# A retention, mixture-of-experts and Mish kernel: x's rows at one place in 256 bytes, one weight rounded later, Mish in the first activation

## The chip, the cores and the metric

The kernel runs on one core of a Trainium2 chip. The metric is device time in microseconds: the median of the runs, 616.08 us before the change (3 runs, 615.87 to 616.91).

## What is computed

Three stages follow each other; all data are float32 (two inputs of the last stage come as float64).

```python
# 2 batches, 8 heads, 576 positions, 64 dims
scores = scale * np.matmul(q, k.transpose(0, 1, 3, 2))
ret = scores * Dmat[None, :, :, :]          # gamma_h ** (i - j) for i >= j, else 0
attn = np.matmul(ret, v)
x = attn.transpose(0, 2, 1, 3).reshape(1152, 512)
...
for e in range(4):                          # w1[e] 512x1024, w2[e] 1024x512
    h = np.maximum(x @ w1[e], 0.0)
    out += p[:, e:e + 1] * (h @ w2[e])
...
h = out @ w_in                              # 512x2048
g = h * np.tanh(np.log1p(np.exp(np.minimum(h, 20.0))))   # Mish; h itself inside tanh for h > 20
return g @ w_out                            # 2048x512
```

## The kernel before

**Precision.** Every operand of the feed-forward stages is kept as two float32r parts, a rounded high part (ScalarE, a Copy) and the remainder (source minus high part, VectorE or GpSimd). A product of two operands takes three matmuls: high by high, low by high, high by low.

**Retention** (lines 248 to 476) goes through 8 units, each one batch and two heads. For unit u PE makes the scores (L317), the products with v of unit u-1 (L385), the states of the chunks (L351), the last scores (L339), and then `cross(u-1)` (L370, L375), which adds the states' part to the output of unit u-1. `chain(u)` makes the decayed states `sbd`: ScalarE copies the first (L355), VectorE adds the other three (L357). `place_x` and `rest_x` (L395, L402, L407) write the unit's output into x, high and low. Behind the loop stands `cross(7)`, for the last unit. While this goes on, the first weights are prepared: `weight_task` takes the next entry of a list of tasks, which is either the four sums for a weight G (GpSimd, L138 to L141, in place in the raw buffer) or the split of a weight (high part on ScalarE, L162; remainder, L166, in four pieces on GpSimd or in one on VectorE).

**Feed-forward.** The 4 experts make 8 units u = 0 to 7 of 512 hidden columns, and the Mish stage 4 more, u = 8 to 11 (`NE` is 8). Of the 1152 tokens 1024 go in two blocks of 512 and 128 apart. For each unit the list `seq` sets the order:
- S(u,c), c = 0 or 1: the first matrix product, `first_pair`, for 256 hidden columns. The 2x2 block product is done with seven products in place of eight, from sums of x (`xop`, 7 sums of 2 row blocks, high and low) and sums of weights (O as loaded, G summed). One product is 6 matmuls (L227) of 128x128 weights over 512 columns of x. Products 1, 5, 7, 6, 2, 4, 3 accumulate in four PSUM banks; three of them are copied out on ScalarE (L238) before their bank is used on, GpSimd adds two of these (L616, L617), VectorE adds the sums into the banks (L593), and `hidden` turns each finished bank into h: Relu or Mish with a Copy on ScalarE (L570; L566, L567), remainder on VectorE (L571; L568). A bank may be opened by the next S when its remainder is done. S(0,0) runs as `first_plain`, with eight products.
- L(u,c): the same for the last 128 tokens (L655, `xc` stationary), T(u) their second product.
- Y(u,c,tb): the second product (L671 for the experts, L687 for the Mish stage), 24 matmuls of 512 columns, added into `acc`.

The first S of the Mish stage, S(8,0), takes the products in the order 1, 5, 7, 3, 6, 2, 4, since the sums of x for it come late. Then follow L(8,1), S(8,1), Y(8,0,0), Y(8,1,0), S(9,0), L(9,0), Y(8,0,1), Y(8,1,1), T(8) and S(9,1).

The engines' orders are as written: each engine takes its instructions in the order in which the Python code issues them. Behind every step but S, `feed_forward` calls `task` once (`catch_up` gives another number and engine at some steps), and a list `later` puts some tasks into the middle of the next S, behind product 7. Raw weights are loaded by the SyncE queue (`load_w`, L130) into three buffers, each load waiting until the buffer's last reader is done; the float64 weights of the Mish stage are turned into float32 on VectorE and ScalarE (L507 to L533) between the rest and go out to DRAM and back.

The lines that the change touches: the tile of x (L197 to L199, SBUF padded to 32 bytes), the dummy activation before the first matmul (L416), the task of unit 6 of retention (L459), `hidden` (L563 to L573), `first_pair` (L609 to L632), and `task` and `catch_up` (L803 to L852).

Of the kernel before, what the change touches and what calls it, by code (L numbers as in the profile page):

```python
# [77 lines left out]
def f32(ap):  # L78
    return ap.bitcast(F32)
# [3 lines left out]
def retention_moe_mish(ctx: ExitStack, tc: tile.TileContext, kq_in, kv_in, probs, w1, w2, w64, cdec, out):  # L83
# [112 lines left out]

    xop = keep.tile([P, 2, 7, 2, TB + 16], F32R, tag="x", name="x")[..., :TB]  # L197
    xc = keep.tile([P, 2, NPAIR, LT], F32R, tag="xc", name="xc")
    p_last = keep.tile([P, E], F32, tag="pl", name="pl")  # L199

# [47 lines left out]
    with ExitStack() as actx:  # L248
# [160 lines left out]
        def retention():  # L409
# [4 lines left out]
            for i, val in enumerate((-896.0, 255.0, 255.0 * 2 ** 23)):  # L414
                dve.memset(cbias[:, i:i + 1], val)
            act.activation(out=acc[:, 0, :1], in_=cbias[:, :1], func=AF.Copy)  # L416
            warm = ps_tile()
# [8 lines left out]
            for u in range(NUN):  # L426
# [30 lines left out]
                if u == 3:  # L457
                    sp.dma_start(out=p_dram.rearrange("e (n t) -> n e t", t=PT), in_=pt)
                for _ in range({2: 1, 5: 1, 6: 1}.get(u, 0)):  # L459
                    weight_task(u - NUN - 2, pool)  # L460
# [101 lines left out]

    def hidden(u, out, src):  # L563

        if u >= NE:
            act.activation(out=src, in_=src, func=AF.Mish)  # L566
            act.activation(out=out[:, 0], in_=src, func=AF.Copy)  # L567
            dve.tensor_tensor(out=out[:, 1], in0=src, in1=f32(out[:, 0]), op=ALU.subtract)  # L568
            return
        act.activation(out=out[:, 0], in_=src, func=AF.Relu)  # L570
        dve.scalar_tensor_tensor(  # L571
            out=out[:, 1], in0=src, scalar=0.0, in1=f32(out[:, 0]), op0=ALU.max, op1=ALU.subtract
        )  # L573

# [12 lines left out]
    def first_pair(u, c, behind, later, order, sum_at=7):  # L587

        o = [[bank(t, j) for j in range(2)] for t in range(2)]
        h = [h_tile(u, c, i) for i in range(2)]  # L590

        def add(out, a, b):
            dve.tensor_tensor(out=out, in0=a, in1=b, op=ALU.add)  # L593

        done = {}
        for n in order:
            done[n] = product(u, c, n, o)
            if n == 1:
                p1 = copy_sum("p1", sums, done[n])
            elif n == 5:  # L600
                p5 = copy_sum("p5", sums, done[n])
            elif n == 7:
                p7 = copy_sum("p7", ph, done[n])
                if 2 in done:
                    hidden(u, h[0][:, :, 0], done[2])
            elif n == 6:
                p16 = sum_tile("p16", ph)
                add(p16, done[n], p1)
            elif n == 2 and 7 in done:  # L609
                if 3 in done:  # L610
                    add(done[3], done[3], p16)
                hidden(u, h[0][:, :, 0], done[2])
                if 3 in done:
                    hidden(u, h[1][:, :, 0], done[3])
            if n == sum_at:
                pool.tensor_tensor(out=p5, in0=p5, in1=p7, op=ALU.add)  # L616
                pool.tensor_tensor(out=p5, in0=p5, in1=p1, op=ALU.add)  # L617
            if n == 7:
                while later:
                    later.pop(0)()  # L620
            for f in behind.get(n, ()):
                f()
            if n == 4:
                add(done[4], done[4], p16)
                hidden(u, h[0][:, :, 1], done[4])
            if len(done) == 7:
                if n == 3:
                    add(done[3], done[3], p16)
                add(done[6], done[6], p5)
                if n == 3:  # L630
                    hidden(u, h[1][:, :, 0], done[3])
                hidden(u, h[1][:, :, 1], done[6])  # L632

# [148 lines left out]
    def feed_forward():  # L782
# [19 lines left out]
        for i, (m, u, *at) in enumerate(seq):  # L802
            def task(n=1, lo_engine=pool):  # L803
                for _ in range(n):
                    weight_task(i, lo_engine)

            if m == "S":
# [13 lines left out]
                elif (u, c) == (0, 1):  # L821
                    later.append(lambda: task(2))
                elif u == NE:
                    later.append(lambda: task(1))
                    later.append(lambda: task(2, dve))
                elif c == 1:
                    later.append(task)
                if (u, c) == (0, 0):
                    first_plain(u, c, behind)
                    task(2)  # L830
                else:
                    first_pair(u, c, behind, later, order, sum_at)
# [15 lines left out]

            catch_up = {("Y", 0, 0, 0): (2, dve), ("L", 1, 0): (1, dve), ("Y", 0, 0, 1): (2, pool)}
            catch_up |= {("Y", NE, 0, 0): (2, dve), ("L", NE + 1, 0): (1, dve), ("Y", NE, 0, 1): (2, dve)}  # L850
            if m != "S" and i != i_x and not i_x + 2 <= i <= i_x + 4:
                task(*catch_up.get(seq[i], (1, pool)))  # L852
            if m != "S":
# [68 lines left out]
```

## Time and profile before

| | |
|---|---|
| median of 3 runs | 616.08 us (615.87 to 616.91) |
| the profiled execution | 615.17 us |
| its span | 613.3 us |
| PE matmul busy | 601.5 us, 98% |
| PE weight loads busy | 500.7 us, 82% |
| VectorE (DVE) busy | 430.6 us, 70% |
| GpSimd (POOL) busy | 368.7 us, 60% |
| ScalarE (ACT) busy | 310.6 us, 51% |

A busy time of PE holds the overlap and the waits between pipelined matmuls, so 98% does not say how fast the matmuls follow each other: their pace is read from their starts. Times in the rows are microseconds from the span's start. In a timeline row stand the start, the length, the engine, the line, the operation, out<-in, the shape and the number of merged instructions, and in brackets how long the engine stood idle before and what ended that.

### The profile page before, as it was taken

How to read it: one execution, taken by the hardware profiler on the slowest of the kernel's cores; microseconds unless marked ns; L12 is line 12 of the kernel's file. 1: busy time of each engine (PE TensorE's matmuls, PEld its weight loads, DVE VectorE, ACT ScalarE, POOL GpSimd, SP SyncE). 2: the span in 40 equal slices, each digit the busy share in tenths (PEclk: the TensorE clock that was granted, in tenths of full speed). 3: DMA queues.
4: the chain of work that ended last, by engine and by line, in shares of the span. 5: the costliest groups of instructions: out<-in, count | busy, mean ns of one | idle time of the engine just before them, and what ended most of it. 6: DMA issues, size and time to landing. Idle time of an engine off the chain costs nothing.

```text
span 613.3 us, 8553 instructions
## 1 busy us (share of the span) xinstructions
PE 601.5 (98%) x3189; PEld 500.7 (82%) x3189; DVE 430.6 (70%) x568; ACT 310.6 (51%) x472; POOL 368.7 (60%) x413
## 2 busy tenths in 40 slices
PE   8979999999999999999999999999899999999997
PEld 7968888888888888888888888888778788888886
DVE  3857569779779779779779879769566867344133
ACT  3646356455455546546545545425656665345130
POOL 2471738948848847857856856773551775854300
PEclk9989999999999999999999999999999999999999
DMA  8934213532631632631632641631220541220023
GB/s 336 397 105 118 90 34 124 180 109 91 203 119 56 203 120 70 223 120 52 204 122 69 214 116 67 187 71 52 61 77 12 194 120 53 85 69 1 0 69 120
DMA packets 56801, 72.30 MB, mean 118 GB/s; under 512 B 31160, under 2 KB 38456, under 8 KB 56760
## 3 DMA queue, kind: packets, MB, share of 16 engines
q1 hardware_dynamic: 56616, 71.46, 36.4%
q8 instruction: 25, 0.41, 0.3%
q10 hardware_dynamic: 144, 0.29, 0.1%
q14 instruction: 16, 0.13, 0.1%
HBM read 57.57 MB, written 14.17 MB: 117 GB/s over the span
## 4 chain that ended last, share of the span: by engine, by line
PE 83%; DMA 5%; POOL 4%; DVE 3%; issue 2%; ACT 2%; SPq 0%; POOLq 0%; DVEq 0%
PE b L227 33%; PE ps L671 28%; PE ps L687 17%; PE ps L655 5%; DMA kq<-kq_in 2%; DMA wr<-w 2%; POOL w L166 1%; DMA cst_sb<-cdec 1%; DMA w<-w 1%; POOL p L616 1%; POOL x L728 1%; POOL qg L302 0%; DVE acc L745 0%; ACT h L567 0%; DVE ps L744 0%
## 5 line engine op out<-in xcount | busy, mean ns | idle before, releaser
L166 POOL TENSOR_TENSOR w<-wr,w 128x256 fp32r<-128x256 f32 x252 | 214.0, 882 | 135.1 <-ACT w L162 135.1
L227 PE MATMUL b<-x,w 128*128 128x512 f32 x1014 | 240.8, 395 | 2.0 <-DVE h L568 1.6
L227 PEld LDWEIGHTS b<-x,w 128*128 128x128 f32 x1014 | 190.3, 188 | 47.2 <-DVE h L568 2.5
L671 PE MATMUL ps<-h,w 128*128 128x512 f32 x768 | 177.0, 389 | 0.0
L671 PEld LDWEIGHTS ps<-h,w 128*128 128x128 f32 x768 | 143.2, 188 | 29.4 <-issue 0.3
L687 PE MATMUL ps<-w,h 128*128 128x512 f32 x384 | 88.6, 390 | 0.2 <-POOL w L166 0.2
L162 ACT ACTIVATE w<-wr 128x1024 fp32r<-128x1024 f32 x71 | 73.8, 1053 | 27.3 <-POOL wr L141 27.0
L687 PEld LDWEIGHTS ps<-w,h 128*128 128x128 f32 x384 | 71.6, 188 | 15.2 <-POOL w L166 0.6
L238 ACT ACTIVATE p<-b 128x512 f32<-128x512 f32 x69 | 40.6, 598 | 52.9 <-PE b L227 52.7
L570 ACT ACTIVATE h<-b 128x512 fp32r<-128x512 f32 x64 | 38.0, 597 | 56.4 <-DVE b L593 44.2
L571 DVE SCALAR_TENSOR_TENSOR h<-b,h 128x512 fp32r<-128x512 f32 x64 | 42.8, 689 | 30.1 <-ACT h L570 28.5
L616 POOL TENSOR_TENSOR p<-p,p 128x512 f32<-128x512 f32 x23 | 34.2, 1486 | 22.6 <-ACT p L238 22.6
L593 DVE TENSOR_TENSOR b<-b,p 128x512 f32<-128x512 f32 x69 | 45.7, 691 | 2.5 <-POOL p L617 2.0
L744 DVE TENSOR_TENSOR ps<-ps,pb 128x1024 f32<-128x1024 f32 x28 | 34.4, 1229 | 16.5 <-PE ps L671 16.4
L568 DVE TENSOR_TENSOR h<-b,h 128x512 fp32r<-128x512 f32 x32 | 22.1, 691 | 30.4 <-ACT h L567 30.4
L519 ACT ACTIVATE e<-e,cbias 128x512 uint32<-128x512 uint32 x32 | 23.0, 718 | 34.1 <-DVE e L507 34.1
L655 PEld LDWEIGHTS ps<-w,xc 128*128 128x128 f32 x288 | 37.2, 188 | 1.9
L655 PE MATMUL ps<-w,xc 128*128 128x256 f32 x288 | 37.8, 280 | 0.0
L530 DVE SCALAR_TENSOR_TENSOR g<-w,g 128x512 f32<-128x512 uint32 x32 | 36.0, 1125 | 0.0
L745 DVE TENSOR_TENSOR acc<-acc,ps 128x1024 f32<-128x1024 f32 x28 | 34.2, 1221 | 1.0
L687 PE MATMUL ps<-w,hl 128*128 128x512 f32 x144 | 34.6, 389 | 0.0
L593 DVE TENSOR_TENSOR p<-b,p 128x512 f32<-128x512 f32 x23 | 15.8, 685 | 26.0 <-PE b L227 19.7
(79 smaller groups left out, 596.8 us busy)
## 6 DMA issues: line engine op xcount, KB each, us to landing
wr<-w SPq DMA_DIRECT2D x32, 512.0 KB, 5.2
w<-w SPq DMA_DIRECT2D x32, 512.0 KB, 4.5
O<-g SPq DMA_DIRECT2D x16, 256.0 KB, 5.4
W<-g SPq DMA_DIRECT2D x16, 256.0 KB, 4.7
wr<-O SPq DMA_DIRECT2D x8, 512.0 KB, 3.5
wr<-W SPq DMA_DIRECT2D x8, 512.0 KB, 3.5
kq<-kq_in SPq DMA_DIRECT2D x7, 576.0 KB, 9.2
kv<-kv_in SPq DMA_DIRECT2D x7, 544.0 KB, 9.3
```

The source lines that it names most:

```text
L162: act.activation(out=w[:, 0], in_=t, func=AF.Copy)
L166: lo_engine.tensor_tensor(out=w[:, 1, k], in0=t[:, k], in1=f32(w[:, 0, k]), op=ALU.subtract)
L227: pe.matmul(o[t][j], w[:, a, 2 * kh + kk, fb * P:(fb + 1) * P], xop[:, b, r, kk], start=opens and i == 0, stop=i == 5, skip_group_check=no ...
L238: act.activation(out=t, in_=src, func=AF.Copy)
L530: dve.scalar_tensor_tensor(out=g, in0=lo_w, scalar=2.0 ** -52, in1=g, op0=ALU.mult, op1=ALU.add)
L570: act.activation(out=out[:, 0], in_=src, func=AF.Relu)
L571: dve.scalar_tensor_tensor(out=out[:, 1], in0=src, scalar=0.0, in1=f32(out[:, 0]), op0=ALU.max, op1=ALU.subtract)
L593: dve.tensor_tensor(out=out, in0=a, in1=b, op=ALU.add)
L616: pool.tensor_tensor(out=p5, in0=p5, in1=p7, op=ALU.add)
L655: pe.matmul(o, xc[:, b, k], w[:, a, k], start=k == 0 and n == 0, stop=k == 3 and n == 2)
L671: pe.matmul(o[:, j], w[:, a, d:d + P], h[:, b, f], start=i == f == n == 0, stop=i == f == 1 and n == 2,)
L687: pe.matmul(o[:, n], h, w[:, b, f * DM:(f + 1) * DM], start=k == f == i == 0, stop=k == f == 1 and i == 2,)
```

## The change

It does five things.
1. The tile of x loses its 16 elements of padding per row (2112 bytes become 2048), and `p_last`, 16 bytes padded to 32, is allocated ahead of it. In the built program x's rows start at 192, 0, 64 and 128 past a multiple of 256 bytes before, and all at 224 now; `xc` goes from 192 to 224. The weights, h, `hl` and `acc` lie at 224 before and after.
2. The split of the weight G of S(0,1), the third weight in the list of tasks, moves from unit 6 of retention to behind the last `rest_x`.
3. The dummy activation at the start is Mish in place of Copy; the program then has one ACT_TABLE_LOAD, where it had two.
4. `hidden` is cut into a high part (ScalarE) and a low part (VectorE). In S(8,0) alone this gives another order: VectorE's adds into the banks of products 4 and 6 come before the low parts of the banks of 3 and 4. The other S keep their order.
5. `task` takes a list of engines. Behind Y(8,0,0) one of two remainders goes to GpSimd, behind L(9,0) and Y(8,0,1) all of them; before they went to VectorE.

```diff
-    xop = keep.tile([P, 2, 7, 2, TB + 16], F32R, tag="x", name="x")[..., :TB]
+    p_last = keep.tile([P, E], F32, tag="pl", name="pl")
+    xop = keep.tile([P, 2, 7, 2, TB], F32R, tag="x", name="x")
     xc = keep.tile([P, 2, NPAIR, LT], F32R, tag="xc", name="xc")
-    p_last = keep.tile([P, E], F32, tag="pl", name="pl")
...
-            act.activation(out=acc[:, 0, :1], in_=cbias[:, :1], func=AF.Copy)
+            act.activation(out=acc[:, 0, :1], in_=cbias[:, :1], func=AF.Mish)
...
-                for _ in range({2: 1, 5: 1, 6: 1}.get(u, 0)):
+                for _ in range({2: 1, 5: 1}.get(u, 0)):
                     weight_task(u - NUN - 2, pool)
...
             rest_x(NUN - 1)
+            weight_task(-1, pool)
...
-    def hidden(u, out, src):
+    def hidden_high(u, out, src):
         if u >= NE:
             act.activation(out=src, in_=src, func=AF.Mish)
             act.activation(out=out[:, 0], in_=src, func=AF.Copy)
+        else:
+            act.activation(out=out[:, 0], in_=src, func=AF.Relu)
+
+    def hidden_low(u, out, src):
+        if u >= NE:
             dve.tensor_tensor(out=out[:, 1], in0=src, in1=f32(out[:, 0]), op=ALU.subtract)
...
+            elif n == 2 and 3 in done:
+                add(done[3], done[3], p16)
+                h2, h3 = (u, h[0][:, :, 0], done[2]), (u, h[1][:, :, 0], done[3])
+                hidden_high(*h2)
+                hidden_high(*h3)
+                hidden_low(*h2)
             elif n == 2 and 7 in done:
-                if 3 in done:
-                    add(done[3], done[3], p16)
                 hidden(u, h[0][:, :, 0], done[2])
-                if 3 in done:
-                    hidden(u, h[1][:, :, 0], done[3])
...
             if n == 4:
                 add(done[4], done[4], p16)
-                hidden(u, h[0][:, :, 1], done[4])
+                h4, h6 = (u, h[0][:, :, 1], done[4]), (u, h[1][:, :, 1], done[6])
+                hidden_high(*h4)
+                hidden_low(*(h3 if 3 in done else h4))
             if len(done) == 7:
...
-                hidden(u, h[1][:, :, 1], done[6])
+                hidden_high(*h6)
+                if n == 4:
+                    hidden_low(*h4)
+                hidden_low(*h6)
...
-            def task(n=1, lo_engine=pool):
-                for _ in range(n):
+            def task(*engines):
+                for lo_engine in engines or (pool,):
                     weight_task(i, lo_engine)
...
-                    later.append(lambda: task(1))
-                    later.append(lambda: task(2, dve))
+                    later.append(lambda: task(pool, dve, dve))
...
-            catch_up = {("Y", 0, 0, 0): (2, dve), ("L", 1, 0): (1, dve), ("Y", 0, 0, 1): (2, pool)}
-            catch_up |= {("Y", NE, 0, 0): (2, dve), ("L", NE + 1, 0): (1, dve), ("Y", NE, 0, 1): (2, dve)}
+            catch_up = {("Y", 0, 0, 0): (dve, dve), ("L", 1, 0): (dve,), ("Y", 0, 0, 1): (pool, pool)}
+            catch_up |= {("Y", NE, 0, 0): (dve, pool), ("Y", NE, 0, 1): (pool, pool)}
```

How it moves the instructions, at the three places that count. On ACT, at the end of retention, before (`sbd_107` is the state tile of the last unit, `w` and `wr` the split and the raw weight):

```order
L402 ACTIVATE xc<-acc 128x128
L402 ACTIVATE x<-acc 128x512
L162 ACTIVATE w<-wr 128x1024
L355 ACTIVATE sbd_107<-b_606 128x64
L395 ACTIVATE acc<-ps 128x576
...
L722 ACTIVATE x<-acc 128x2x512 x3
```

And on ACT at the same place now:

```order
L402 ACTIVATE xc<-acc 128x128
L402 ACTIVATE x<-acc 128x512
L355 ACTIVATE sbd_107<-b_600 128x64
L395 ACTIVATE acc<-ps 128x576
L402 ACTIVATE x<-acc 128x512
...
L162 ACTIVATE w<-wr 128x1024
L738 ACTIVATE x<-acc 128x1024 x3
```

The copy L162 has moved from ahead of `sbd` to behind the unit's placing, ahead of the first three high parts of x's sums (L722 before, L738 now).

On DVE in S(8,0) before, from the add of products 6 and 1 on (`b_3864`, `b_3866`, `b_3865` and `b_3867` are the banks of h2, h3, h4 and h6):

```order
L593 TENSOR_TENSOR b_3866<-b_3866,p_3914 128x512
L568 TENSOR_TENSOR h<-b_3864,h 128x512
L568 TENSOR_TENSOR h<-b_3866,h 128x512
L593 TENSOR_TENSOR b_3865<-b_3865,p_3914 128x512
L568 TENSOR_TENSOR h<-b_3865,h 128x512
L593 TENSOR_TENSOR b_3867<-b_3867,p_3886 128x512
L568 TENSOR_TENSOR h<-b_3867,h 128x512
```

The same stretch of DVE now:

```order
L602 TENSOR_TENSOR b_3866<-b_3866,p_3914 128x512
L574 TENSOR_TENSOR h<-b_3864,h 128x512
L602 TENSOR_TENSOR b_3865<-b_3865,p_3914 128x512
L574 TENSOR_TENSOR h<-b_3866,h 128x512
L602 TENSOR_TENSOR b_3867<-b_3867,p_3886 128x512
L574 TENSOR_TENSOR h<-b_3865,h 128x512
L574 TENSOR_TENSOR h<-b_3867,h 128x512
```

Each add of a bank now stands ahead of the low part of the bank before it; ACT's order there is the same but for the table load.

On POOL from S(8,1) to S(9,0) and on, before (`wr` the sums of a G in place, `p` the sums of copied products):

```order
L166 TENSOR_TENSOR w<-wr,w 128x256 x4
L138 TENSOR_TENSOR wr<-wr 128x2x128
...
L617 TENSOR_TENSOR p_4165<-p_4165,p_4157 128x512
L138 TENSOR_TENSOR wr<-wr 128x2x128
L139 TENSOR_TENSOR wr<-wr 128x2x128
L140 TENSOR_TENSOR wr<-wr 128x2x128
L141 TENSOR_TENSOR wr<-wr 128x2x128
L166 TENSOR_TENSOR w<-wr,w 128x256 x8
```

And on POOL now:

```order
L141 TENSOR_TENSOR wr<-wr 128x2x128
L166 TENSOR_TENSOR w<-wr,w 128x256 x4
L138 TENSOR_TENSOR wr<-wr 128x2x128
...
L628 TENSOR_TENSOR p_4168<-p_4168,p_4160 128x512
L166 TENSOR_TENSOR w<-wr,w 128x256 x8
L138 TENSOR_TENSOR wr<-wr 128x2x128
L139 TENSOR_TENSOR wr<-wr 128x2x128
L140 TENSOR_TENSOR wr<-wr 128x2x128
L141 TENSOR_TENSOR wr<-wr 128x2x128
L166 TENSOR_TENSOR w<-wr,w 128x256 x8
```

Four pieces have come ahead of the second group of sums, and eight (two weights) ahead of the third, behind the sums of S(9,0)'s products; three L166 of 128x1024 have gone from DVE.

## Rows read from the trace of the kernel before

**Rows 1.** Waits of PE: line waited for, us in total, times, longest us.

```profile
PE ps L370 <- ACT sbd L355: 3.7, 1, 3.7
...
PE ps L687 <- POOL w L166: 0.2, 1, 0.2
```

**Rows 2.** Stretches of 1 us: busy us of each engine, then TensorE's granted clock.

```profile
39.00:40.00 1.00, 0.00 (x0) 0.00 (x0) 0.00 (x0) 0.69 (x1) 0.28 (x1) 1.00 0.00 0
...
41.00:42.00 1.00, 1.00 (x14) 1.00 (x12) 0.96 (x4) 0.65 (x2) 1.00 (x3) 0.50 0.00 0
```

**Rows 3.** Timeline, the end of retention, ACT, DVE and PE.

```profile
34.23 0.61 ACT L402 ACTIVATE x<-acc 128x512 fp32r<-128x512 f32 x1
...
35.85 1.09 PE L385 MATMUL ps<-ret,kv 128*64 128x128 f32 x16
...
39.31 1.06 ACT L162 ACTIVATE w<-wr 128x1024 fp32r<-128x1024 f32 x1 [4.47 <-POOL wr L141]
...
40.51 0.91 DVE L357 SCALAR_TENSOR_TENSOR sbd<-sbd,cst_sb,b 128x64 f32<-128x64 f32 x3 [5.21 <-ACT sbd L355]
...
40.62 1.76 PE L370 MATMUL ps<-qg,sbd 64*64 64x128 f32 x16 [3.68 <-ACT sbd L355]
...
42.52 9.24 PE L227 MATMUL b<-x,w 128*128 128x512 f32 x36
```

**Rows 4.** Timeline of PE from S(1,0) on, and the page's group of L227.

```profile
77.85 9.89 PE L227 MATMUL b<-x,w 128*128 128x512 f32 x42
...
87.58 1.57 PE L655 MATMUL ps<-w,xc 128*128 128x256 f32 x12
...
88.99 11.05 PE L671 MATMUL ps<-h,w 128*128 128x512 f32 x48
...
99.88 0.39 PE L687 MATMUL ps<-w,hl 128*128 128x512 f32 x1
...
L227 PE MATMUL b<-x,w 128*128 128x512 f32 x1014 | 240.8, 395 | 2.0 <-DVE h L568 1.6
```

**Rows 5.** Timeline, S(8,0) to S(8,1), ACT, DVE and PE.

```profile
426.90 1.28 ACT L566 ACT_TABLE_LOAD   x1
...
429.07 0.58 ACT L566 ACTIVATE b<-b 128x512 f32<-128x512 f32 x1 [0.89 <-PE b L227]
...
431.66 2.95 PE L227 MATMUL b<-x,w 128*128 128x512 f32 x12
431.96 0.69 DVE L568 TENSOR_TENSOR h<-b,h 128x512 fp32r<-128x512 f32 x1 [0.70 <-ACT h L567]
...
433.29 0.58 ACT L566 ACTIVATE b<-b 128x512 f32<-128x512 f32 x1 [1.36 <-DVE b L593]
...
434.53 0.69 DVE L568 TENSOR_TENSOR h<-b,h 128x512 fp32r<-128x512 f32 x1 [1.28 <-ACT h L567]
...
435.28 1.66 PE L227 MATMUL b<-x,w 128*128 128x512 f32 x6 [0.67 <-DVE h L568]
...
437.86 5.82 PE L227 MATMUL b<-x,w 128*128 128x512 f32 x24 [0.92 <-DVE h L568]
```

**Rows 6.** Timeline, Y(8,0,1) to S(9,1), with POOL's eight pieces of L166 twice.

```profile
469.81 2.00 ACT L162 ACTIVATE w<-wr 128x1024 fp32r<-128x1024 f32 x2
...
477.07 0.74 POOL L138 TENSOR_TENSOR wr<-wr 128x256 f32<-128x256 f32 x1 [14.44 <-DVE w L166]
...
479.64 5.73 PE L227 MATMUL b<-x,w 128*128 128x512 f32 x24
...
480.63 1.06 ACT L162 ACTIVATE w<-wr 128x1024 fp32r<-128x1024 f32 x1 [3.44 <-POOL wr L141]
...
481.77 7.43 POOL L166 TENSOR_TENSOR w<-wr,w 128x256 fp32r<-128x256 f32 x8 [1.17 <-ACT w L162]
...
485.82 4.41 PE L227 MATMUL b<-x,w 128*128 128x512 f32 x18 [0.45 <-ACT p L238]
...
527.11 5.63 POOL L166 TENSOR_TENSOR w<-wr,w 128x256 fp32r<-128x256 f32 x8 [1.17 <-ACT w L162]
```

More of the change, by code (lines that the diff above doesn't have):

```diff
@@ L567, in hidden @@
             act.activation(out=out[:, 0], in_=src, func=AF.Copy)
+        else:
+            act.activation(out=out[:, 0], in_=src, func=AF.Relu)
+    def hidden_low(u, out, src):
+        if u >= NE:
             dve.tensor_tensor(out=out[:, 1], in0=src, in1=f32(out[:, 0]), op=ALU.subtract)
[L569 to L573, printed above, removed]
+        else:
+            dve.scalar_tensor_tensor(
+                out=out[:, 1], in0=src, scalar=0.0, in1=f32(out[:, 0]), op0=ALU.max, op1=ALU.subtract
+            )
+    def hidden(*args):
+        hidden_high(*args)
+        hidden_low(*args)
     def first_plain(u, c, behind):
@@ L821, in feed_forward @@
                 elif (u, c) == (0, 1):
-                    later.append(lambda: task(2))
+                    later.append(lambda: task(pool, pool))
                 elif u == NE:
-                    later.append(lambda: task(1))
-                    later.append(lambda: task(2, dve))
+                    later.append(lambda: task(pool, dve, dve))
                 elif c == 1:
@@ L829, in feed_forward @@
                     first_plain(u, c, behind)
-                    task(2)
+                    task(pool, pool)
                 else:
@@ L847, in feed_forward @@
             ahead = i + 1 < len(seq) and seq[i + 1][0] == "S"
-            catch_up = {("Y", 0, 0, 0): (2, dve), ("L", 1, 0): (1, dve), ("Y", 0, 0, 1): (2, pool)}
-            catch_up |= {("Y", NE, 0, 0): (2, dve), ("L", NE + 1, 0): (1, dve), ("Y", NE, 0, 1): (2, dve)}
+            catch_up = {("Y", 0, 0, 0): (dve, dve), ("L", 1, 0): (dve,), ("Y", 0, 0, 1): (pool, pool)}
+            catch_up |= {("Y", NE, 0, 0): (dve, pool), ("Y", NE, 0, 1): (pool, pool)}
             if m != "S" and i != i_x and not i_x + 2 <= i <= i_x + 4:
-                task(*catch_up.get(seq[i], (1, pool)))
+                task(*catch_up.get(seq[i], ()))
             if m != "S":
```

## The prediction

> **What bounds the kernel now.** I read the list of waits first. In a span of 613.3 us TensorE (PE) waits long only once, 3.7 us at the end of retention, for `sbd` of ScalarE (ACT); its shortest listed wait is 0.2 us for a weight of GpSimd (POOL) [rows 1]. So PE is the bound, and a change pays only where it shortens PE's own work, or one of its few waits. Second, the clock in small windows: behind the 3.7 us the granted clock is 0.50, which is the 1.2 GHz level, where 1.00 (2.4 GHz) stood before [rows 2]; that wait costs more than its length. Third, the timeline, read for PE's pace. From the first of 42 matmuls of L227 (x moving) to the next row 9.73 us pass, 231.7 ns each; from the first of 48 of L671 (h moving) to the next row 10.89 us, 226.9 ns [rows 4]. Both move 512 columns over a 128x128 weight tile and wait for nothing. What differs is where the moving rows lie: in the built program the weights and h start 224 bytes past a multiple of 256, x's rows at 192, 0, 64 and 128, since a row is 528 elements long. Last, the timeline around the other waits [rows 5, 6].
>
> **Part A, x's place.** With rows of 512 elements and `p_last` ahead, all rows of x begin at 224. No instruction is added or moved. The nearest row for a matmul with both operands at 224 is L671, with the same form and type, so I take its pace: 231.7 - 226.9 = 4.8 ns less, times the 1014 matmuls of L227 [rows 4], 4.9 us, all on the path. The ends: 0 if the place is not the cause (below), and 6 us if x gets a nanosecond below h. `xc` moves from 192 to 224 as well, as the stationary operand of L655: 1.41 us for 12, 117.5 ns [rows 4]. At the 2.4 GHz level 256 columns take 106.7 ns and 512 take 213.3, so L655 has 10.8 ns beyond its columns, L671 13.6; L655 has nothing to give by that comparison. I take 0, with 0.7 us (half of the 4.8 ns on 288) as the end.
>
> **Part B, G(0,1) rounded behind retention.** ACT's copy L162 of that weight stands ahead of L355, which starts `sbd` of the last unit. It idles 4.47 us for POOL's sums and runs from 39.31 to 40.37; L355 follows, DVE's three L357 start at 40.51, and PE's L370 at 40.62 [rows 3]. Without it, L355 runs when ACT has done L402 at 34.84: 0.21 us more, then 0.91 of L357, so `sbd` is there by 36.0. PE's L385 ends at 35.85 + 1.09 = 36.94 [rows 3]. So L370 starts there, 40.62 - 36.94 = 3.7 us sooner, 0.9 us behind its operand. The clock then has no reason to fall: L370 and L375 (40.62 to 42.52, 1.90 us at half clock) save 0.95, and the 36 matmuls from 42.52, 9.24 us where 35 x 0.2317 + 0.395 = 8.50 would do, save 0.74 [rows 2 to 4]. B is 3.68 + 0.95 + 0.74 = 5.4 us. The ends: 4.4, if the clock falls for another reason, and 5.8. The moved copy (1.06 us) now stands on ACT ahead of the three L722 that round T1, T3 and T2; those wait for DVE's L713, which needs the last x, so they lose nothing. POOL's four remainders follow at about 41 to 44.5. Product 5 of S(0,1) is the first to read G(0,1), 54 matmuls of L227 and 24 of L655 after PE starts S(0,0) at about 38, so at 53: 8 us of cover. SP's next raw load into that buffer waits for POOL to about 44.5; it is a weight of S(1,0), behind S(0,1) and 48 matmuls of L671.
>
> **Part C, halves of h in S(8,0).** Mish of h4 cannot start before DVE's add, and that add stood behind the low half of h3, which idles 0.70 us for ACT and starts at 431.96 [rows 5]. Now the add comes first, from about 431.3 to 432.0: Mish of h4 starts at 432.0 in place of 433.29, and its low half, 1.24 us behind as now (433.29 to 434.53), at 433.3, done at 434.0. The add of h6 follows h3's low half, its Mish starts at 433.3 and its low half ends at 435.3. PE without waits would want the first bank at 431.66 + 12 x 0.2317 = 434.4 and the second at 435.8. Both waits go, with 0.4 us over: 435.28 - 431.66 = 3.62 becomes 2.78, and 437.86 - 435.28 = 2.58 becomes 1.39 [rows 5], 2.0 us together. The ends: 1.0, if the second wait stays, and 2.2.
>
> **Part D, Mish in the dummy.** The second table load takes 1.28 us at 426.90, but then ACT idles another 0.89 for PE at 429.07 [rows 5]. Its removal is worth 0; were that cover gone, 1.28 us.
>
> **Part E, three remainders from DVE to POOL.** Around S(9,1) PE waits for a copy of product 1 (L238), which on ACT stands behind L162 of G(10,0), which waits for POOL's sums. 24 matmuls take 485.82 - 479.64 = 6.18 us where 5.56 would do, 0.62 lost [rows 6]. The sums began at 477.07, after POOL had idled 14.44 us for DVE's remainder, and ended 3.5 us later, when L162 starts at 480.63. Now POOL makes the eight pieces itself, from ACT's first copy at 470.8. Eight pieces took 5.63 us where DVE was idle, 7.43 beside DVE [rows 6]. So they end at 476.4 or 478.2, and the sums 0.6 us sooner or 1.2 later than now. DVE has 2.4 us less to do in that stretch, so I take the middle, 6.53: the wait grows by 0.3. The rule that bears on it: the Trainium skill (SBUF — State Buffer, section "SBUF: two separate sides") says that a DVE instruction with two SBUF inputs and a GpSimd instruction that reads SBUF shut each other out for a whole instruction. By it alone every piece here that meets one would go at the slower rate; the two rows for eight pieces agree with it, 5.63 against 7.43. The third remainder goes to POOL behind Y(8,0,0), ahead of sums that wait for this very remainder; they feed S(9,1), a whole S and two Y later: 0. PE's 0.2 us for POOL [rows 1] has the same POOL work ahead of it as before, so it stays.
>
> **Sum:** 4.9 + 5.4 + 2.0 + 0 - 0.3 = 12.0 us. The profiled execution took 615.17, so 603.2; the median of the runs, 616.08, is 0.9 above it, so **604.1**.
>
> **Rivals.**
> 1. *The place does not matter.* x's matmuls may be slower for another reason, such as their PSUM banks being read meanwhile. Against it: L671 runs beside the same engines at a steady 226.9 [rows 4]. Then A is 0 and the gain 7.1: 609.0. The Trainium skill (SBUF — State Buffer, section "A bandwidth-pool intuition that's wrong (but worth ruling out)") would have it so, with a second, independent read port for weight loads; no run here has moved x yet.
> 2. *POOL takes the place of DVE.* If the eight pieces take 7.43 and the sums stretch alike (3.5 to 4.6), L162 starts 2.3 us later, and so does PE. It decides from 6.3 us for the eight on (470.8 to 477.07) [rows 6]. For it: DVE works there. The sum is 12.3 - 2.3 = 10.0: 606.1.
> 3. *The wait at retention's end stays,* because something else is late there, such as `qg`, which POOL makes. B is 0: 609.5. Against it, the 0.9 us that `sbd` has to spare [rows 3].
> 4. *Slower: equal places collide.* If moving rows and weights at the same place were read against each other, L227 would slow down. It decides when it loses all of B, C and E and 1.2 us more, 8.3 us, that is 8.2 ns a matmul, at 239.9 ns; at 243 the gain of 7.1 turns into 1014 x 11.3 = 11.5 lost, 620.5. Against it stands L671, which has equal places and is the fastest [rows 4].
>
> **How the numbers follow.** The forecast has 0.72, the rivals 0.10, 0.12, 0.03 and 0.03 in their order. The range takes in rival 2 and half of A's loss, to 607.6, and the better ends of A, B, E and `xc` in part, to 601.4; rivals 1, 3 and 4, and 0.04 of tails, lie outside. A measurement of this kernel can tell 0.2%, 1.2 us, from no change. All but rival 4 are faster than that; allowing 0.02 for several shortfalls at once, 0.95 faster, 0.02 the same, 0.03 slower.
>
> **What would show it.** A: 42 matmuls of x in about 9.53 us from their first to the next row. B: no PE wait for `sbd`, S(0,0) starting near 38 us, a granted clock of 1.00 through 36 to 45. C: no PE wait for a low half of h. D: one table load. E: the copy L162 before S(9,1)'s second half within 1.2 us of the sums' place now, and PE's wait for L238 between 0 and 2 us. The prediction is wrong if x's pace stays above 230 ns, if PE still idles over 1 us before S(0,0), or if a new wait for POOL of over 2.5 us appears after S(8,1).

## The result, and the profile after

| | before | after |
|---|---|---|
| median of the runs (4 each, taken together) | 616.50 us | **608.54 us** (606.91 to 609.06) |
| ratio | | 0.9867, 95% interval 0.9844 to 0.9890 |
| the profiled execution | 615.17 us | 608.04 us |
| its span | 613.3 us | 606.3 us |

The kernel became faster, by 8.0 us where 12.0 were forecast: 608.5 lies above the range. Three of the four runs took 608.0 to 609.1 at a mean granted clock of 0.996 or 0.997, the fourth 606.91 at 1.000. The lines below the edits have moved: L655, L671 and L687 of before are L671, L687 and L703 now, L568 is L574, L571 is L576 and L593 is L602. VectorE's conversions L507, L511, L527, L530 and L533 are L508, L512, L528, L531 and L534 now, its eviction L776 is L792, and its sums of x, L713 and L719, are L729 and L735.

First the page after: its first line, and the group of x's matmuls (busy us, mean ns of one, idle before).

```profile
span 606.3 us, 8562 instructions
...
L227 PE MATMUL b<-x,w 128*128 128x512 f32 x1014 | 236.7, 391 | 3.3 <-ACT p L238 2.9
```

Then the waits of PE after (us in total, times, longest), which answer to [rows 1].

```profile
PE b L227 <- ACT p L238: 2.9, 1, 2.9
...
PE b L227 <- DVE h L576: 0.4, 1, 0.4
```

The 3.7 us for `sbd` are gone, and so are the two waits of S(8,1). A wait of 2.9 us for a copy on ACT has come, where [rows 6] had 0.45, and one of 0.4 us at S(0,1).

**Pace of PE and S(8,1).** The timeline of PE after, from S(1,0) on, against [rows 4], and at S(8,1), against [rows 5].

```profile
72.62 9.68 PE L227 MATMUL b<-x,w 128*128 128x512 f32 x42
82.14 1.59 PE L671 MATMUL ps<-w,xc 128*128 128x256 f32 x12
83.57 11.07 PE L687 MATMUL ps<-h,w 128*128 128x512 f32 x48
94.48 2.88 PE L703 MATMUL ps<-w,hl 128*128 128x512 f32 x12
...
423.96 9.71 PE L227 MATMUL b<-x,w 128*128 128x512 f32 x42
...
433.51 11.36 PE L703 MATMUL ps<-w,h 128*128 128x512 f32 x48
```

42 matmuls of x go by in 82.14 - 72.62 = 9.52 us, 226.7 ns each, at the pace of h beside them (48 of 128x512 from 83.57 to 94.48, 227.3 each, 226.9 before). The 12 matmuls with `xc` take 1.43, 119.2 ns, where they took 117.5. S(8,1) goes through its 42 matmuls in 9.55 us without a wait.

**The end of retention.** The timeline after, PE, ACT, DVE and POOL, against [rows 3].

```profile
36.57 0.99 PE L370 MATMUL ps<-qg,sbd 64*64 64x128 f32 x16
...
37.61 8.45 PE L227 MATMUL b<-x,w 128*128 128x512 f32 x36
...
39.96 1.07 ACT L162 ACTIVATE w<-wr 128x1024 fp32r<-128x1024 f32 x1 [0.72 <-POOL wr L141]
...
41.10 6.15 POOL L166 TENSOR_TENSOR w<-wr,w 128x256 fp32r<-128x256 f32 x4 [1.18 <-ACT w L162]
...
43.22 1.76 DVE L735 TENSOR_TENSOR x<-acc,x 128x1024 fp32r<-128x1024 f32 x1
...
51.51 1.55 PE L227 MATMUL b<-x,w 128*128 128x512 f32 x6
...
53.45 6.87 PE L227 MATMUL b<-x,w 128*128 128x512 f32 x29 [0.39 <-DVE h L576]
```

PE starts S(0,0) at 37.61 without a pause ahead of it, and the granted clock is 1.00 in all of the stretches from 34 to 52. But POOL's four pieces take 6.15 us, 1.5 each on average, beside DVE's sums of x; before the change they took 3.29, ahead of these sums. The sums are longer too: an L735 takes 1.76 us here and 1.22 at 50.41. DVE is late, and S(0,1) waits: six matmuls take 53.45 - 51.51 = 1.94 us in place of 1.36.

**S(9,1).** The timeline after from L(9,0) on, against [rows 6].

```profile
459.52 2.00 ACT L162 ACTIVATE w<-wr 128x1024 fp32r<-128x1024 f32 x2
...
460.65 7.75 POOL L166 TENSOR_TENSOR w<-wr,w 128x256 fp32r<-128x256 f32 x8 [8.31 <-ACT w L162]
...
463.49 0.96 DVE L508 TENSOR_SCALAR e<-w 128x512 uint32<-128x512 uint32 x1
...
468.48 0.74 POOL L138 TENSOR_TENSOR wr<-wr 128x256 f32<-128x256 f32 x1
...
469.29 1.07 POOL L139 TENSOR_TENSOR wr<-wr 128x256 f32<-128x256 f32 x1
469.37 5.60 PE L227 MATMUL b<-x,w 128*128 128x512 f32 x24
469.69 1.22 DVE L531 SCALAR_TENSOR_TENSOR g<-w,g 128x512 f32<-128x512 uint32 x1
...
472.69 1.06 ACT L162 ACTIVATE w<-wr 128x1024 fp32r<-128x1024 f32 x1 [5.44 <-POOL wr L141]
...
477.24 1.55 ACT L238 ACTIVATE p<-b 128x512 f32<-128x512 f32 x3
...
477.87 5.98 PE L227 MATMUL b<-x,w 128*128 128x512 f32 x18 [2.90 <-ACT p L238]
...
483.68 1.59 PE L671 MATMUL ps<-w,xc 128*128 128x256 f32 x12
```

POOL's eight pieces take 7.75 us. They are not alike in the trace: the three beside DVE's L528, L531 and L534, which read two inputs each, take 1.18 to 1.23 us, the four beside its L508 and L512, which read one input, 0.92 or 0.93, and the one beside the eviction L792 alone 0.74. From the pieces' first row to the sums' first row 7.83 us pass, then 4.21 to ACT's copy at 472.69. From ACT's first copy to this one it is 13.17 us, where it was 480.63 - 469.81 = 10.82. The copies of PE's products (L238 at 477.24) stand on ACT behind it, four conversions and a second L162, and PE loses 477.87 - 469.37 - 24 x 0.2269 = 3.05 us. What follows is slow as well: 18 matmuls take 483.68 - 477.87 = 5.81 us in place of 4.08. The reason is in the stretches of 1 us there (busy us of PE, PEld, DVE, ACT, POOL, then the granted clock):

```profile
477.00:478.00 1.00, 0.13 (x1) 0.13 (x2) 0.97 (x3) 1.00 (x3) 0.59 (x1) 1.00 0.38 90
478.00:479.00 1.00, 1.00 (x4) 0.82 (x5) 1.00 (x2) 1.00 (x3) 1.00 (x2) 0.72 0.86 225
479.00:480.00 1.00, 1.00 (x4) 0.81 (x3) 0.51 (x1) 0.74 (x1) 1.00 (x2) 0.50 0.84 315
...
482.00:483.00 1.00, 1.00 (x6) 0.79 (x5) 0.79 (x2) 0.00 (x0) 0.92 (x2) 1.00 0.83 291
```

Behind the wait the clock falls to 0.50, the 1.2 GHz level, and is back at 1.00 some 4 us later, as it did behind the 3.7 us of before [rows 2].

### The profile page after: what moved, and what is told of

Its sections match the earlier page's. It is cut to its first block, busy times and chain, and to the rows that moved or that the text cites. A ratio compares the mean times of both kernels' runs of the same rounds, so it can differ in the third digit from the quotient of the medians.

```text
span 606.3 us, 8562 instructions
## 1 busy us (share of the span) xinstructions
PE 598.0 (99%) x3189; PEld 501.4 (83%) x3189; DVE 440.1 (73%) x565; ACT 309.0 (51%) x471; POOL 381.3 (63%) x425
## 4 chain that ended last, share of the span: by engine, by line
PE 80%; POOL 6%; DVE 4%; DMA 3%; issue 3%; ACT 2%; SPq 0%; POOLq 0%; ACTq 0%; DVEq 0%
PE b L227 31%; PE ps L687 27%; PE ps L703 16%; PE ps L671 4%; POOL w L166 3%; DMA cst_sb<-cdec 3%; DVE acc L729 2%; POOL p L627 1%; PE ps L370 1%; DVE x L735 1%; PE ps L385 1%; DMA kq<-kq_in 1%; POOL x L744 1%; PE b L317 1%; ACT w L162 1%
## 5 line engine op out<-in xcount | busy, mean ns | idle before, releaser
L166 POOL TENSOR_TENSOR w<-wr,w 128x256 fp32r<-128x256 f32 x264 | 224.1, 880 | 138.3 <-ACT w L162 138.3
L227 PE MATMUL b<-x,w 128*128 128x512 f32 x1014 | 236.7, 391 | 3.3 <-ACT p L238 2.9
L227 PEld LDWEIGHTS b<-x,w 128*128 128x128 f32 x1014 | 190.9, 189 | 43.8 <-ACT p L238 3.3
L687 PE MATMUL ps<-h,w 128*128 128x512 f32 x768 | 177.2, 390 | 0.0
L687 PEld LDWEIGHTS ps<-h,w 128*128 128x128 f32 x768 | 143.3, 188 | 29.5 <-issue 0.3
L703 PE MATMUL ps<-w,h 128*128 128x512 f32 x384 | 88.6, 390 | 0.0
L162 ACT ACTIVATE w<-wr 128x1024 fp32r<-128x1024 f32 x71 | 73.8, 1053 | 25.5 <-POOL wr L141 25.3
L703 PEld LDWEIGHTS ps<-w,h 128*128 128x128 f32 x384 | 71.6, 188 | 15.0 <-POOL w L166 0.4
L238 ACT ACTIVATE p<-b 128x512 f32<-128x512 f32 x69 | 40.3, 596 | 50.1 <-PE b L227 49.9
L576 DVE SCALAR_TENSOR_TENSOR h<-b,h 128x512 fp32r<-128x512 f32 x64 | 42.7, 688 | 25.4 <-ACT h L570 24.4
L602 DVE TENSOR_TENSOR b<-b,p 128x512 f32<-128x512 f32 x69 | 45.6, 689 | 3.2 <-POOL p L628 2.9
L574 DVE TENSOR_TENSOR h<-b,h 128x512 fp32r<-128x512 f32 x32 | 22.1, 690 | 29.1 <-ACT h L568 29.1
L671 PEld LDWEIGHTS ps<-w,xc 128*128 128x128 f32 x288 | 37.7, 191 | 1.9
L671 PE MATMUL ps<-w,xc 128*128 128x256 f32 x288 | 38.3, 283 | 0.0
L534 DVE TENSOR_TENSOR g<-g,e 128x512 f32<-128x512 f32 x32 | 36.4, 1136 | 1.1
L531 DVE SCALAR_TENSOR_TENSOR g<-w,g 128x512 f32<-128x512 uint32 x32 | 36.0, 1124 | 0.0
L703 PE MATMUL ps<-w,hl 128*128 128x512 f32 x144 | 34.7, 390 | 0.0
```

The costliest lines, as they stand in the source:

```text
L162: act.activation(out=w[:, 0], in_=t, func=AF.Copy)
L166: lo_engine.tensor_tensor(out=w[:, 1, k], in0=t[:, k], in1=f32(w[:, 0, k]), op=ALU.subtract)
L227: pe.matmul(o[t][j], w[:, a, 2 * kh + kk, fb * P:(fb + 1) * P], xop[:, b, r, kk], start=opens and i == 0, stop=i == 5, skip_group_check=no ...
L238: act.activation(out=t, in_=src, func=AF.Copy)
L534: dve.tensor_tensor(out=g, in0=g, in1=e.bitcast(F32), op=ALU.mult)
L576: dve.scalar_tensor_tensor(out=out[:, 1], in0=src, scalar=0.0, in1=f32(out[:, 0]), op0=ALU.max, op1=ALU.subtract)
```

## The experiments

Each was timed against the kernel before on the same chip. The edits are against the kernel after or before, as said; the ratio is to before.

**1. The change without E.** After, with the three remainders back on VectorE:

```diff
-            catch_up |= {("Y", NE, 0, 0): (dve, pool), ("Y", NE, 0, 1): (pool, pool)}
+            catch_up |= {("Y", NE, 0, 0): (dve, dve), ("L", NE + 1, 0): (dve,), ("Y", NE, 0, 1): (dve, dve)}
```

> The changed kernel with part E undone alone: the remainders behind Y(8,0,0), L(9,0) and Y(8,0,1) go to VectorE again. Theory 1 (GpSimd's eight pieces and the sums behind them are what makes PE wait 2.9 us in S(9,1), and that wait drops the clock): the wait falls to 0 to 0.7 us, the granted clock stays at 1.00 there, and the time is about 604.2 us, 4.3 us below the changed kernel. Theory 2 (the wait comes from the rest of the change, which brings PE to S(9,1) earlier than the float64 conversion can follow): PE still waits about 3 us there, and the time stays near 608.5.

605.45 us (604.85 to 605.85), ratio 0.9815 [0.9802, 0.9828]. E cost 3.1 us in the whole, by the medians; theory 1's 604.2 was 1.2 too low. PE's wait at S(9,1) is back at 0.6, and the granted clock stays at 1.00 there. Timeline of that run, DVE and PE:

```profile
464.05 0.68 DVE L531 SCALAR_TENSOR_TENSOR g<-w,g 128x512 f32<-128x512 uint32 x1
...
465.37 0.42 DVE L508 TENSOR_SCALAR e<-w 128x512 uint32<-128x512 uint32 x1
...
466.04 1.22 DVE L792 COPY acc<-ps 128x1024 f32<-128x1024 f32 x1
...
468.26 2.88 PE L703 MATMUL ps<-w,hl 128*128 128x512 f32 x12
...
477.23 4.37 PE L227 MATMUL b<-x,w 128*128 128x512 f32 x18 [0.64 <-ACT p L238]
```

**2. E alone**, on the kernel before: `task` and `catch_up` as in the change, the rest as it was.

> The kernel before with part E alone. Theory 1 (E by itself makes the wait in S(9,1)): GpSimd's eight pieces end some 7.7 us after the first copy, the sums take about 4.2, PE's wait grows from 0.45 to about 3 us, the clock falls behind it, and the time is 619 to 621. Theory 2 (E hurts only together with the faster rest): within 1 us of before.

620.19 us, ratio 1.0067 [1.0049, 1.0084], against 616.04: 4.15 us lost. Timeline row of PE and two of the stretches of 1 us behind its wait:

```profile
488.66 6.00 PE L227 MATMUL b<-x,w 128*128 128x512 f32 x18 [2.74 <-ACT p L238]
```

```profile
489.00:490.00 1.00, 1.00 (x4) 0.80 (x3) 1.00 (x2) 1.00 (x3) 1.00 (x2) 0.55 0.87 246
...
493.00:494.00 1.00, 1.00 (x6) 0.81 (x5) 0.91 (x2) 0.00 (x0) 1.00 (x1) 1.00 0.94 360
```

The same wait and the same fall of the clock, without A to D: it is E's doing, and not a meeting with the other parts.

**3. E without the remainder of L(9,0)**, which stays on VectorE:

```diff
-            catch_up |= {("Y", NE, 0, 0): (dve, pool), ("Y", NE, 0, 1): (pool, pool)}
+            catch_up |= {("Y", NE, 0, 0): (dve, pool), ("L", NE + 1, 0): (dve,), ("Y", NE, 0, 1): (pool, pool)}
```

> The changed kernel, but the remainder behind L(9,0) goes to VectorE again; those behind Y(8,0,0) and Y(8,0,1) stay on GpSimd. Theory 1 (it is the length of GpSimd's queue ahead of the sums: eight pieces, 7.75 us, and sums stretched to 4.2): with four pieces the sums end some 3 us sooner, PE's wait in S(9,1) goes, 603.5 to 604.2 us. Theory 2 (it is the sums' own contention with VectorE's conversions, whenever they run): the wait shrinks to 1 to 2 us at most, 605 to 607.

605.78 us, ratio 0.9820 [0.9807, 0.9832], where theory 1 had 603.5 to 604.2. With four pieces in place of eight ahead of the sums, the wait at S(9,1) is gone. But a new one of 1.5 us has come at T(8), for VectorE's eviction L792. Timeline of that run, PE, DVE and POOL:

```profile
462.38 4.27 POOL L166 TENSOR_TENSOR w<-wr,w 128x256 fp32r<-128x256 f32 x4 [9.25 <-ACT w L162]
...
463.69 1.22 DVE L531 SCALAR_TENSOR_TENSOR g<-w,g 128x512 f32<-128x512 uint32 x1
...
467.74 1.21 DVE L792 COPY acc<-ps 128x1024 f32<-128x1024 f32 x1
...
469.01 3.06 PE L703 MATMUL ps<-w,hl 128*128 128x512 f32 x12 [1.48 <-DVE acc L792]
```

In run 1, where POOL stood idle there, L528 and L531 took 0.69 and 0.68 us, and here 1.23 and 1.22; L508 and L512, with one input, took 0.42 each there and 0.96 here. So both engines pay for the meeting: a piece of POOL 1.07 us on average, and counted from the start of the remainder ahead of it (L166 on VectorE), the eviction L792 starts 2.6 us later than in run 1, 1.1 of them through L508 and L512.

**4. The remainder of Y(8,0,0) alone on GpSimd:**

```diff
-            catch_up |= {("Y", NE, 0, 0): (dve, pool), ("Y", NE, 0, 1): (pool, pool)}
+            catch_up |= {("Y", NE, 0, 0): (dve, pool), ("L", NE + 1, 0): (dve,), ("Y", NE, 0, 1): (dve, dve)}
```

> Of part E only the remainder behind Y(8,0,0) goes to GpSimd; the ones behind L(9,0) and Y(8,0,1) stay on VectorE; parts A to D as changed. Theory 1 (this remainder costs nothing, as the prediction had it, and the whole loss of E comes from the eight pieces ahead of the last sums): 605.4, PE's wait at S(9,1) 0.6 us, no new wait above 0.3. Theory 2 (the delay is handed on from the second group of sums to the third): PE's wait at S(9,1) or a wait before Y(8,0,1) grows to 1 us or more and the time is 606 or more.

**604.59 us** (604.50 to 605.19), ratio 0.9806 [0.9790, 0.9823], the lowest median of all. This third of E costs nothing; whether it gains over run 1 the intervals don't tell. The whole loss comes from the two remainders ahead of the last sums, and it takes both: run 3, with one of them on GpSimd, is near run 1.

**5. E undone, and the second remainder earlier on VectorE:**

```diff
-            catch_up |= {("Y", NE, 0, 0): (dve, pool), ("Y", NE, 0, 1): (pool, pool)}
+            catch_up |= {("Y", NE, 0, 0): (dve, dve), ("L", NE + 1, 0): (dve, dve), ("Y", NE, 0, 1): (pool,)}
```

> Part E undone, as in the run that took 605.45, but VectorE makes the second of the two remainders in front of Y(8,0,1) directly behind the first, ahead of its conversions L528 to L534, so that GpSimd's sums start some 5 us sooner. Theory 1 (PE's wait at S(9,1) is set by the end of these sums, whichever engine makes the remainder): that wait, 0.64 us, goes; VectorE's evictions L792 ahead of T(8) come 1.2 us later, or more where the sums stretch VectorE's own instructions, and PE waits 0.2 to 1.0 us there: 604.9 to 605.8, about 605.4. Theory 2 (the wait is set by something else, such as ScalarE's own queue): it stays at 0.6 us and the time is 605.6 to 606.5.

608.90 us (606.09 to 609.54): a miss. Its timeline, ACT, DVE, POOL and PE:

```profile
463.49 1.12 POOL L138 TENSOR_TENSOR wr<-wr 128x256 f32<-128x256 f32 x1 [10.69 <-DVE w L166]
463.92 1.23 DVE L531 SCALAR_TENSOR_TENSOR g<-w,g 128x512 f32<-128x512 uint32 x1
...
467.97 1.21 DVE L792 COPY acc<-ps 128x1024 f32<-128x1024 f32 x1
...
469.24 3.06 PE L703 MATMUL ps<-w,hl 128*128 128x512 f32 x12 [2.06 <-DVE acc L792]
469.88 1.04 ACT L162 ACTIVATE w<-wr 128x1024 fp32r<-128x1024 f32 x1
```

The sums start early and the wait at S(9,1) is gone, so theory 1's mechanism holds. But the sums now run beside VectorE's conversions, and the eviction starts 0.8 us after PE wanted T(8) (469.24 - 2.06 = 467.18), where in run 1 it started 2.2 us before (466.04 against 468.26). Counted from the start of the first remainder it comes 3.2 us later than in run 1; 1.1 of these are the second remainder, and 2.0 the conversions, which are longer beside the sums. T(8) waits 2.06 us, twice what was allowed. Its five runs fall in two groups: 606.09 and 606.79 at a mean granted clock of 1.000, 608.90 to 609.54 at 0.997. The profile is of the first group, and shows no fall of the clock behind the wait. Where the second group lost its 3 us is not shown: no trace of it was taken, and the mean clock does not tell, since the four runs of run 4, two at 0.997 and two at 1.000, all took 604.50 to 605.19.

**6. A alone**, on the kernel before (rows of 2048 bytes and `p_last` ahead), and **7. equal rows at another place** (`p_last` left behind; x and `xc` at 192, the weights at 224):

```diff
+    p_last = keep.tile([P, E], F32, tag="pl", name="pl")
-    xop = keep.tile([P, 2, 7, 2, TB + 16], F32R, tag="x", name="x")[..., :TB]
+    xop = keep.tile([P, 2, 7, 2, TB], F32R, tag="x", name="x")
     xc = keep.tile([P, 2, NPAIR, LT], F32R, tag="xc", name="xc")
-    p_last = keep.tile([P, E], F32, tag="pl", name="pl")
```

> The kernel before with x's rows at 224 past a multiple of 256 and nothing else. Theory 1 (the place is the cause of the slower pace): L227 falls from 231.7 to 226.9 ns a matmul, the time by 4.9 us to about 611.5. The pace of the products with xc stationary, which moves to 224 too, rises from 117.5 to 119.3 ns as in the changed kernel, 0.5 us of it given back. Theory 2 (the faster pace of the changed kernel comes from elsewhere, as from fewer VectorE readers): no change, 616.3.

> The kernel before with rows of 2048 bytes but no tile moved ahead: all rows of x and xc lie at 192, the weights at 224. Theory 1 (the moving rows must lie where the weights lie): L227 stays at 231 to 234 ns, the time within 2 us of before. Theory 2 (it is enough that all rows of x lie alike, since a change of place from one matmul to the next costs): 227 ns, 611.5 us.

A alone: 612.90 us against 616.66, ratio 0.9936 [0.9922, 0.9950], 3.8 us less by the medians; the interval allows 3.1 to 4.8. Run 7 (the same diff without its lines on `p_last`): 617.77, ratio 1.0016 [1.0007, 1.0025]. PE's timeline at S(1,0), first A alone, then run 7:

```profile
77.98 9.68 PE L227 MATMUL b<-x,w 128*128 128x512 f32 x42
87.50 1.59 PE L655 MATMUL ps<-w,xc 128*128 128x256 f32 x12
```

```profile
78.82 9.96 PE L227 MATMUL b<-x,w 128*128 128x512 f32 x42
88.63 1.56 PE L655 MATMUL ps<-w,xc 128*128 128x256 f32 x12
```

9.52 us for 42 matmuls at 224, 226.7 ns, and 9.81 at 192, 233.6. Equal row lengths bring nothing; the place does.

**8. All operands at 0** (run 1, with `cbias` 32 bytes longer):

```diff
-    cbias = keep.tile([P, 16], F32, tag="cbias", name="cbias")
+    cbias = keep.tile([P, 24], F32, tag="cbias", name="cbias")
```

> The change without part E, with cbias made 32 bytes longer: x, xc, the weights, h, hl and acc then all lie at 0 past a multiple of 256 bytes in place of 224. Theory 1 (what counts is the place of the moving rows relative to the weights' place): L227 stays at 226.9 ns a matmul, 605.4. Theory 2 (what counts is the moving rows' own place, and 0 is worth what x's rows at 0 had before, 229.7 ns): L227 at 229.7, 605.4 + 1014 x 2.8 ns = 608.3, and more if h slows as well.

605.04 us (604.44 to 605.24), ratio 0.9811 [0.9792, 0.9830]. PE's timeline:

```profile
72.93 9.68 PE L227 MATMUL b<-x,w 128*128 128x512 f32 x42
82.45 1.60 PE L671 MATMUL ps<-w,xc 128*128 128x256 f32 x12
```

Again 9.52 us for 42. At 0 with the weights at 224, x's matmuls had gone at 229.7 ns before: it is the place relative to the weights' that counts.

**9. B alone**, on the kernel before:

```diff
-                for _ in range({2: 1, 5: 1, 6: 1}.get(u, 0)):
+                for _ in range({2: 1, 5: 1}.get(u, 0)):
...
             rest_x(NUN - 1)
+            weight_task(-1, pool)
```

> The kernel before with part B alone: G(0,1) is split behind retention. Theory 1 (the wait for sbd and the half clock behind it are worth 5.4 us): no wait of PE before S(0,0), granted clock 1.00 from 36 to 45 us, and about 611.3 us. Theory 2 (GpSimd's four remainders now meet VectorE's sums of x, so a low half of h comes late): a new wait of PE of about 0.4 us at S(0,1), 0.65 us with the refill, and about 611.9.

610.85 us, ratio 0.9913 [0.9896, 0.9931]: 5.2 us less than 616.04. PE does not wait for `sbd` any more, and no wait at S(0,1) is listed, where theory 2 had 0.4.

**10. Run 1 without C**: `hidden` and the adds in S(8,0) in the order of before.

```diff
-            elif n == 2 and 3 in done:
-                add(done[3], done[3], p16)
-                h2, h3 = (u, h[0][:, :, 0], done[2]), (u, h[1][:, :, 0], done[3])
-                hidden_high(*h2)
-                hidden_high(*h3)
-                hidden_low(*h2)
             elif n == 2 and 7 in done:
+                if 3 in done:
+                    add(done[3], done[3], p16)
                 hidden(u, h[0][:, :, 0], done[2])
+                if 3 in done:
+                    hidden(u, h[1][:, :, 0], done[3])
...
-                h4, h6 = (u, h[0][:, :, 1], done[4]), (u, h[1][:, :, 1], done[6])
-                hidden_high(*h4)
-                hidden_low(*(h3 if 3 in done else h4))
+                hidden(u, h[0][:, :, 1], done[4])
...
-                hidden_high(*h6)
-                if n == 4:
-                    hidden_low(*h4)
-                hidden_low(*h6)
+                hidden(u, h[1][:, :, 1], done[6])
```

> The changed kernel with parts E and C undone. Theory 1 (C is worth the two waits of PE for a low half of h in S(8,1)): both waits are back, 0.8 and 1.2 us with the refill, and the time is about 607.5, 2.0 us above the kernel without E alone. Theory 2 (with x's faster pace and the early table load the waits are hidden anyway): 605.5.

607.22 us, ratio 0.9854 [0.9839, 0.9869]. PE's timeline:

```profile
427.71 1.66 PE L227 MATMUL b<-x,w 128*128 128x512 f32 x6 [0.82 <-DVE h L574]
430.28 5.73 PE L227 MATMUL b<-x,w 128*128 128x512 f32 x24 [0.92 <-DVE h L574]
```

Both waits are back, 0.82 and 0.92 us. C is worth 1.8 us by the medians of this run and run 1, and 2.4 by the rows: the 42 matmuls of S(8,1) take 435.86 - 423.95 = 11.91 us here and 9.55 after.

**11. D alone**, on the kernel before, with Mish in the dummy activation:

```diff
-            act.activation(out=acc[:, 0, :1], in_=cbias[:, :1], func=AF.Copy)
+            act.activation(out=acc[:, 0, :1], in_=cbias[:, :1], func=AF.Mish)
```

> The kernel before with part D alone: Mish in the dummy activation. Theory 1 (the second table load lay under a wait of ScalarE for PE): the time of before, 616.1, within 0.3. Theory 2 (it held up S(8,0)): up to 1.28 us less, 614.8.

616.67 us, ratio 1.0002 [0.9992, 1.0011]. The table load lay under a wait.

**12. Run 1 with G(0,1)'s remainder on VectorE, and `xc` at 192**:

```diff
+    keep.tile([P, 56], F32, tag="gap0", name="gap0")
     xc = keep.tile([P, 2, NPAIR, LT], F32R, tag="xc", name="xc")
+    keep.tile([P, 8], F32, tag="gap1", name="gap1")
...
-            weight_task(-1, pool)
+            weight_task(-1, dve)
```

> The changed kernel without E, with two more edits: the remainder of G(0,1) behind retention on VectorE in one piece, and xc back at 192 past a multiple of 256 (224 unused bytes behind x, 32 behind xc). Theory 1 (GpSimd's pieces slow VectorE's sums of x more than the one piece would, and xc is better off at 192): no wait of PE at S(0,1), 117.5 ns a matmul with xc stationary, 604.3 us, 1.1 below the kernel without E. Theory 2 (VectorE is the one that is late there, so its own piece costs as much as the meeting): the wait at S(0,1) stays at 0.2 to 0.5 us, 605.0.

605.06 us, ratio 0.9819 [0.9803, 0.9834], the same as run 1. The `xc` product gained its 0.5 us (46.48 to 47.88 below, 1.40), but the wait at S(0,1) grew from 0.18 to 0.58: VectorE is the late engine there, and with its remainder of 1.23 us ahead, the sums of x start 4.40 us behind S(0,0) (42.57 and 38.17), where in run 1 they start 2.59 behind it (41.30 and 38.71). By these two traces that costs more than POOL's pieces beside them do; but the traces after and of run 4, with the same code there as run 1, have a wait of 0.39, so the difference is not clear of the spread. PE's timeline (the lines are two higher here):

```profile
46.48 1.56 PE L673 MATMUL ps<-w,xc 128*128 128x256 f32 x12
47.88 2.92 PE L229 MATMUL b<-x,w 128*128 128x512 f32 x12
...
54.17 4.19 PE L229 MATMUL b<-x,w 128*128 128x512 f32 x17 [0.58 <-DVE h L578]
```

## Why the prediction was right and wrong

The forecast of the profiled execution was 603.2, and it took 608.04. The 4.8 us are found in the rows of after.

- **A, right.** 4.8 ns on each matmul of x were forecast and 231.7 - 226.7 = 5.0 measured. Rival 1 falls with run 6, rival 4 too. Run 6 gained 3.8 us by the medians, where 4.9 less 0.5 for `xc` would be 4.4; its interval holds both. The Trainium skill (SBUF — State Buffer, section "A bandwidth-pool intuition that's wrong (but worth ruling out)") lists a second, independent read port for weight loads; by that alone the place of x relative to the weights would not matter, and runs 6 to 8 differ from it (226.7, 233.6 and 226.7 ns). `xc` was taken as 0 and costs 1.7 ns on 288 matmuls, **0.5 us**, inside the end of 0.7.
- **B, right in its main part:** 5.4 forecast, 5.2 measured alone. The cover of the weight held: it is done at 47.25, and product 5 of S(0,1) starts at 53.45. But the four remainders were put at "about 41 to 44.5", and that they meet VectorE's sums of x, which makes the low parts of S(0,0)'s banks late, was not priced. S(0,1) lost 1.94 - 1.36 = **0.6 us**. Run 9, with x at its old pace, lists no wait there; the runs that have A too list between none (run 5) and 0.4 (after, run 4).
- **C and D, right:** 2.0 forecast and 1.8 (medians) or 2.4 (rows) measured for C; 0 forecast for D, and run 11 shows no difference.
- **E is the step that failed.** Its term was +0.3. The rows show 3.05 + 1.73 = 4.78 us lost around S(9,1), 0.69 of which were there before (0.62 ahead of the copy, and behind it 490.06 - 485.82 - 18 x 0.2317 = 0.07): +4.1, **3.8 us** more than forecast.

So 3.8 + 0.6 + 0.5 = 4.9 of 4.8. Differences of half a us and less, of either sign, are left out, such as retention's last units 0.3 us sooner and h's matmuls 0.4 ns slower.

Within E three things were mis-sized. First the eight pieces: between the two rows, 5.63 and 7.43, the middle of 6.53 was taken with the argument that VectorE had 2.4 us less to do. The middle already lay above the 6.3 from which rival 2 was said to decide. It took 7.83 from the first piece to the sums, 1.3 more. VectorE had less to do, but its conversions now stood in just that stretch: three pieces beside L528 to L534 took 3.48 us, where three at 0.70 would be 2.1, and the five beside L508, L512 and L792 took 4.35, where 3.5 would do. Second the sums were kept at 3.5 and took 4.2: in [rows 6] they had stood beside one-input instructions of VectorE (L507, L511, L776), and now they ran into L528 to L534 of the next weight. Rival 2 had both, with ACT's copy 2.3 us later; it came 2.35 later. That the two figures are so close is luck: the rival had 1.2 from the pieces and 1.1 from the sums, and the rows show 1.70 and 0.65. As a mechanism this rival was what happened, at a chance of 0.12. Third, and missing from rival 2 as well: a wait of PE that grows to 2.9 us is followed by matmuls at the lower clock. [Rows 2] showed that behind 3.7 us, and B's term used it; E's range and rival 2's price did not. With these 1.7 us, and the 0.6 and 0.5, rival 2's 606.1 becomes 608.9. The range's upper end of 607.6 takes in rival 2 and half of A's 4.9 one at a time, but not together (608.5). And rival 1's 609.0 lies nearest to the measured time by coincidence, since x's pace rules it out.

The Trainium skill (SBUF — State Buffer, section "SBUF: two separate sides") speaks of VectorE instructions with two SBUF inputs and of GpSimd's as shutting each other out for a whole instruction. The traces agree in that both sides pay: an L140 went from 0.80 us (run 1) to 1.07, a piece of L166 from 0.70 (5.63 / 8) to 0.97 (7.75 / 8) and 1.5 on average, L531 from 0.68 to 1.22, L735 from 1.22 to 1.76. The rows also show a meeting with one input: L508 and L512 went from 0.42 to 0.96, and the pieces beside them took 0.92 or 0.93. The prediction named the rule for two inputs and then took a value halfway between the two rows.

## What to carry to other kernels

Before work is moved from VectorE to GpSimd, list what VectorE will still be doing in the very stretch where GpSimd does it; if work is left there that the traces show to meet it (here the two-input instructions, and also L508 and L512 with one, but not the eviction L792), take the row measured beside a busy VectorE for GpSimd's instructions, lengthen VectorE's by the same meeting, and look whose eviction comes late. A term that makes TensorE wait nearly as long as a wait behind which the trace shows the lower clock should carry the price of that clock too. Where two groups of matmuls of equal shape differ in pace, compare where their moving rows lie relative to the weights.

## What was not expected of the hardware

The pace of an fp32r matmul depends on the places of its two operands relative to each other: 226.7 ns for 512 columns with both at 224 or both at 0, 231.7 over x's four places before (229.7 at 0, 230.8 at 128, 232.9 at 64 and 233.3 at 192, with the weights at 224), 233.6 in run 7 at 192. Where `xc` is the stationary operand and the weights' rows move, it is the other way round: 117 ns for 256 columns with `xc` at 192 and 119 with both at 224. Why is open; no run varied it further.

The granted clock fell behind single waits of PE of 2.6 us (run 7), 2.7 (run 2), 2.9 (after) and 3.7 (before), and not behind the 1.5 us of run 3 or the 2.06 us in the profile of run 5.

VectorE's L508 and L512, with one input each, took 0.96 us beside GpSimd's pieces and 0.42 where GpSimd stood idle; the eviction L792, 1.21 and 1.22, paid nothing.
